# The low part of g in the first block: GpSimd in place of VectorE

## The chip, the cores and the metric

The kernel runs on one core of a Trainium2 chip. The metric is the device time of one execution in microseconds (us). The kernel before took 1154.6 us, the median of three runs (1153.08 to 1154.86). Engines: PE is TensorE (matmuls; PEld its weight loads), DVE is VectorE, ACT is ScalarE, POOL is GpSimd, SP is SyncE, which issues most DMAs.

## The reference

Three layers follow each other, all in float32. Attention works in chunks of 32 queries, each seeing 8 memory keys and a window of 16 + 32 + 8 positions, for 4 batches, 8 heads, 768 positions and a head size of 64. Its output is reshaped to 3072 tokens of 512, and two feed-forward layers follow:

```python
def _moe_ref(x, w_in, w_out):          # x 3072 x 512, w_in 512 x 2048, w_out 2048 x 512
    h = x @ w_in
    g = np.maximum(0.01 * h, h)
    return (g @ w_out).astype(np.float32)

def _moe2_ref(x, w_a, w_b, w_out):     # w_a, w_b 512 x 1536, w_out 1536 x 512
    a = x @ w_a
    b = x @ w_b
    return (a * b @ w_out).astype(np.float32)
```

## The kernel before

TensorE gets its operands split: a float32 value is a high part, the value rounded to float32r by a copy on ScalarE, and a low part, the value less the high part, a subtraction. Each product is three matmuls: low weight by high x, high weight by low x, high by high.

The first feed-forward layer runs over six blocks of 512 tokens (block `bi`, 0 to 5) and in each over 16 slices of 128 hidden units (`f`). An item is one slice of one block. `mm1_pe` makes h (12 matmuls, L412 to L414). `mm1_act` makes g from h on ScalarE (L514) and calls `split_g`: ScalarE casts g to gh (L429), and the subtraction of L430 makes gl. `mm2` multiplies gh and gl with the second weights into four accumulators (12 matmuls, L532, L535, L536). `mm2` of an item comes two items after its `mm1` (`LAG = 2`, list `behind`), so there are two items of matmuls between h and the use of gl.

In block 0 the weights are made as well. A weight arrives as the two 32-bit halves of a float64 pattern. ScalarE scales the high half (L103), VectorE joins the halves in three instructions (L113, L116, L119), ScalarE casts the joined value to the high part (L173), and VectorE subtracts for the low part (L182). Each item of block 0 calls `W1.step()` twice, which makes one first weight (needed by `mm1`) and one second weight (needed by `mm2`). The attention of the next block's four units runs beside the items: scores on TensorE (L276), maxima, differences, sums and products on VectorE (L290, L295, L329 to L332), exponentials on ScalarE (L312), transposes (L356) and the product with v (L385) on TensorE. ScalarE also places q in a padded tile (L248, L249).

The first three items of block 0 have 256 columns, since only half the block's attention is done then; their other halves come as three more items at the end of the block. So block 0 has 3 + 13 + 3 items. The first three are called by `first_items`, where the order on the engines is the written one (class `InOrder`, L31 to L50: each call is issued after the one before; these show the lines L44 and L47 in the profile). After it, `e.on = False`, and the order of each engine's queue is laid out by the framework's planner, which places what it expects to be ready; so instructions of different calls are interleaved in the trace. The queues themselves run in order. GpSimd is called directly, never through `InOrder`, and before the change only for memsets at the start.

The tiles g (tag "t", four buffers), gh and gl (three buffers each) are in SBUF.

Of the kernel before, what the change touches and what calls it, by code (L numbers as in the profile page):

```python
# [53 lines left out]
def kernel(  # L54
# [10 lines left out]
    nc = tc.nc  # L65
# [21 lines left out]
    pe, dve, act, sp = [InOrder(tc, e) for e in (nc.tensor, nc.vector, nc.scalar, nc.sync)]  # L87
# [328 lines left out]
    def proj(ps, slot, x, c):  # L416
        hi, lo = x
        for kc in range(KC):
            mm3(
                ps[:, c],  # L420
                (slot[:, 0, kc * P:kc * P + P], slot[:, 1, kc * P:kc * P + P]),
                (hi[:, kc, c], lo[:, kc, c]),
                kc == 0, kc == KC - 1,
            )

    def split_g(g, c):
        gh = tp.tile([P, TB], F32R, tag="gh", name="gh", bufs=3)
        gl = tp.tile([P, TB], F32R, tag="gl", name="gl", bufs=3)
        act.copy(gh[:, c], g[:, c])  # L429
        dve.tensor_tensor(  # L430
            out=gl[:, c], in0=g[:, c], in1=gh[:, c].bitcast(F32), op=ALU.subtract
        )
        return gh, gl
# [71 lines left out]
    def mm1_pe(bi, parts):  # L505
        ps = ps_h.tile([P, TB], F32, tag="h", name="h")
        for o, n, f in parts:
            proj(ps, wslot[f, 0], x1["x", bi], slice(o, o + n))
        c = slice(min(o for o, _, _ in parts), max(o + n for o, n, _ in parts))
        return ps, c  # L510

    def mm1_act(ps, c):
        g = tp.tile([P, TB], F32, tag="t", name="g")
        act.activation(g[:, c], ps[:, c], AF.Prelu, alpha=0.01)  # L514
        return split_g(g, c)

    def mm1(bi, parts):
        return mm1_act(*mm1_pe(bi, parts))

    def mm2(bi, parts, g):  # L520
        if bi not in acc:
# [32 lines left out]
    for f in range(NF1 + LEAD):  # L554
        if f < LEAD:
            parts = [(0, HALF, f)]
        elif f < NF1:
            parts = [(0, TB, f)]
        else:
            parts = [(HALF, HALF, f - NF1)]  # L560
# [19 lines left out]
    def first_items():  # L580
        parts = [items[f][2] for f in range(LEAD)]
        W1.join()
        a_soft2(2)
        h0 = mm1_pe(0, parts[0])
        g0 = mm1_act(*h0)
        W1.bias(4)
        W1.cast(3)
# [17 lines left out]
        load_v(2)  # L605
        W1.load(13)
        g1 = mm1_act(*h1)
        h2 = mm1_pe(0, parts[2])
        a_turn_mm(3, ps_s, "s")
# [175 lines left out]
    for bi, f, parts in items[LEAD:]:  # L785
# [10 lines left out]
        if first:  # L796
            W1.load(2 * f + 14)
            W1.step()
        behind.append((bi, parts, mm1(bi, parts)))
        if first:  # L800
            W1.step()
# [227 lines left out]
```

## Time and profile before

| | |
|---|---|
| median of three runs | 1154.6 us |
| profiled execution, its own time | 1154.32 us |
| its span | 1152.5 us |
| granted clock of TensorE, mean | 0.998 |
| DVE busy | 665.4 us (58%), 1233 instructions |
| ACT busy | 441.7 us (38%), 734 instructions |
| L430, all blocks | 96 instructions, 65.4 us on DVE |

A row of the timeline gives the start in us from the span's beginning, the duration in us, the engine, the line, the operation, out<-in, shapes and a count, and in brackets the idle time of the engine just before it and what ended that. A row of a stretch gives its length, then busy us and instructions of PE, PEld, DVE, ACT and POOL, TensorE's granted clock, the DMA share and GB/s.

### The profile page before, as it was taken

To read this page: it belongs to the slowest core of one execution; us is meant where nothing else is said; L and a number is where in the kernel's file an instruction comes from. 1 tells how busy PE (TensorE), PEld (TensorE's weight loads), DVE (VectorE), ACT (ScalarE), POOL (GpSimd) and SP (SyncE) were. 2 spreads that over 40 slices of the span, in tenths; PEclk is the share of its full clock that TensorE was granted. 3 is DMA by queue.
4 is the path that set the end of the run, shared out by engine and by line. 5 is a ranking of instruction groups with operands and counts; after the bars stand their busy time and mean duration, and the time that the engine had idled before them with its cause. 6 is when DMAs were issued, how large, how long until landed. Compare 5 with 4: busy or idle time off the path is not lost.

```text
span 1152.5 us, 16036 instructions
## 1 busy us (share of the span) xinstructions
PE 1134.1 (98%) x6344; PEld 938.6 (81%) x6344; DVE 665.4 (58%) x1233; ACT 441.7 (38%) x734; POOL 6.3 (1%) x16
## 2 busy tenths in 40 slices
PE   6899999999999999999999999999999999999998
PEld 6678888888888888888888888888888888888887
DVE  6899489889979834545114433475433465433443
ACT  5787564556455534325223222241222232122210
POOL 2000000000000000000000000000000000000000
PEclk9999999999999999999999999999999999999999
DMA  9977899998999845336248335355544344443413
GB/s 325 354 264 279 308 341 322 317 354 300 330 339 333 298 164 182 111 114 215 92 146 314 144 128 201 128 227 220 208 148 163 146 148 187 185 166 142 186 64 110
DMA packets 68299, 250.67 MB, mean 217 GB/s; under 512 B 7297, under 2 KB 8705, under 8 KB 62849
## 3 DMA queue, kind: packets, MB, share of 16 engines
q1 hardware_dynamic: 67920, 249.33, 60.3%
q8 instruction: 50, 0.82, 0.3%
q10 hardware_dynamic: 304, 0.33, 0.1%
q14 instruction: 25, 0.20, 0.1%
HBM read 200.34 MB, written 49.28 MB: 217 GB/s over the span
## 4 chain that ended last, share of the span: by engine, by line
PE 94%; DVE 0%; DVEq 0%; issue 0%
PE h L412 7%; PE a L532 7%; PE a L536 7%; PE a L535 7%; PE h L414 7%; PE h L413 7%; PE o L925 6%; PE o L927 6%; PE o L926 6%; PE A L860 4%; PE A L859 4%; PE A L858 4%; PE C L858 3%; PE C L860 3%; PE C L859 3%; PE pv L385 2%
## 5 line engine op out<-in xcount | busy, mean ns | idle before, releaser
L412 PE MATMUL h<-xh,w 128*128 128x512 f32 (+1 forms) x384 | 152.1, 396 | 3.1 <-ACT w L47 3.1
L532 PE MATMUL a<-gh,w 128*128 128x512 f32 (+1 forms) x392 | 150.7, 385 | 0.9 <-DVE w L182 0.9
L535 PE MATMUL a<-gl,w 128*128 128x512 f32 (+1 forms) x392 | 150.4, 384 | 0.0
L536 PE MATMUL a<-gh,w 128*128 128x512 f32 (+1 forms) x392 | 150.4, 384 | 0.0
L413 PE MATMUL h<-xl,w 128*128 128x512 f32 (+1 forms) x384 | 149.0, 388 | 0.0
L414 PE MATMUL h<-xh,w 128*128 128x512 f32 (+1 forms) x384 | 148.9, 388 | 0.0
L430 DVE TENSOR_TENSOR gl<-g,gh 128x512 fp32r<-128x512 f32 (+1 forms) x96 | 65.4, 682 | 105.8 <-ACT gh L429 105.6
L925 PE MATMUL o<-w,cl 128*128 128x512 f32 x288 | 112.1, 389 | 0.0
L927 PE MATMUL o<-w,ch 128*128 128x512 f32 x288 | 112.0, 389 | 0.0
L926 PE MATMUL o<-w,ch 128*128 128x512 f32 x288 | 112.0, 389 | 0.0
L514 ACT ACTIVATE g<-h 128x512 f32<-128x512 f32 (+1 forms) x96 | 56.5, 589 | 126.3 <-PE h L414 125.5
L872 ACT COPY u<-A 128x512 f32<-128x512 f32 x72 | 42.3, 588 | 142.2 <-PE A L860 142.2
L412 PEld LDWEIGHTS h<-xh,w 128*128 128x128 f32 x384 | 72.5, 189 | 18.7 <-ACT w L47 3.2
L532 PEld LDWEIGHTS a<-gh,w 128*128 128x128 f32 x392 | 73.7, 188 | 16.3 <-DVE w L182 1.3
L880 DVE TENSOR_TENSOR ga<-u,C 128x512 f32<-128x512 f32 x36 | 24.8, 688 | 106.9 <-ACT u L872 77.7
L536 PEld LDWEIGHTS a<-gh,w 128*128 128x128 f32 x392 | 73.6, 188 | 14.5
L535 PEld LDWEIGHTS a<-gl,w 128*128 128x128 f32 x392 | 73.7, 188 | 14.5
L414 PEld LDWEIGHTS h<-xh,w 128*128 128x128 f32 x384 | 72.4, 189 | 14.8
L859 PE MATMUL A<-cl,wab 128*128 128x512 f32 x216 | 84.1, 389 | 0.0
L858 PE MATMUL A<-ch,wab 128*128 128x512 f32 x216 | 84.0, 389 | 0.0
L860 PE MATMUL A<-ch,wab 128*128 128x512 f32 x216 | 84.0, 389 | 0.0
L413 PEld LDWEIGHTS h<-xl,w 128*128 128x128 f32 x384 | 72.6, 189 | 14.1 <-DVE xl L47 0.3
(138 smaller groups left out, 1918.7 us busy)
## 6 DMA issues: line engine op xcount, KB each, us to landing
wab<-wab SPq DMA_DIRECT2D x36, 1792.0 KB, 7.4
w<-wod SPq DMA_DIRECT2D x116, 512.0 KB, 5.2
raw<-w SPq DMA_DIRECT2D x68, 512.0 KB, 6.9
k<-kl SPq DMA_DIRECT2D x48, 256.0 KB, 5.4
v<-vl SPq DMA_DIRECT2D x48, 256.0 KB, 5.4
wab<-pwb SPq DMA_DIRECT2D x12, 1024.0 KB, 7.7
wab<-pwa SPq DMA_DIRECT2D x12, 768.0 KB, 7.2
wod<-w SPq DMA_DIRECT2D x16, 512.0 KB, 6.1
```

The lines of the kernel that those rows point to most:

```text
L412: pe.matmul(ps, w[1], x[0], start=first, stop=False)
L413: pe.matmul(ps, w[0], x[1], start=False, stop=False)
L414: pe.matmul(ps, w[0], x[0], start=False, stop=last)
L532: pe.matmul(ps, slot[:, 1, c], gh[:, t], start=f == 0 and o == 0, stop=False, **kw)
L535: pe.matmul(ps, slot[:, 0, c], gl[:, t], start=False, stop=False, **kw)
L536: pe.matmul(ps, slot[:, 0, c], gh[:, t], start=False, stop=f == NF1 - 1 or (o == HALF and f == LEAD - 1), **kw)
L858: nc.tensor.matmul(ps, w[:, 1, i, c], hi[:, kc], start=first and kc == 0, stop=False, **kw)
L859: nc.tensor.matmul(ps, w[:, 0, i, c], lo[:, kc], start=False, stop=False, **kw)
L860: nc.tensor.matmul(ps, w[:, 0, i, c], hi[:, kc], start=False, stop=kc == HC - 1, **kw)
L925: nc.tensor.matmul(o, cl[:, q], w[:, 0, :], start=k == 0, stop=False)
L926: nc.tensor.matmul(o, ch[:, q], w[:, 1, :], start=False, stop=False)
L927: nc.tensor.matmul(o, ch[:, q], w[:, 0, :], start=False, stop=k == NCH - 1)
```

## The change

`split_g` takes the engine of the subtraction as an argument. `mm1` passes GpSimd for block 0 and VectorE for the other blocks. The three items of `first_items` call `mm1_act` directly and stay on VectorE. So 16 of the 96 subtractions of L430 move, 13 of 128x512 and 3 of 128x256. All else is as it was.

```diff
-    def split_g(g, c):
+    def split_g(g, c, eng):
         gh = tp.tile([P, TB], F32R, tag="gh", name="gh", bufs=3)
         gl = tp.tile([P, TB], F32R, tag="gl", name="gl", bufs=3)
         act.copy(gh[:, c], g[:, c])
-        dve.tensor_tensor(
+        eng.tensor_tensor(
             out=gl[:, c], in0=g[:, c], in1=gh[:, c].bitcast(F32), op=ALU.subtract
         )
         return gh, gl
...
-    def mm1_act(ps, c):
+    def mm1_act(ps, c, eng=None):
         g = tp.tile([P, TB], F32, tag="t", name="g")
         act.activation(g[:, c], ps[:, c], AF.Prelu, alpha=0.01)
-        return split_g(g, c)
+        return split_g(g, c, eng or dve)
 
     def mm1(bi, parts):
-        return mm1_act(*mm1_pe(bi, parts))
+        return mm1_act(*mm1_pe(bi, parts), nc.gpsimd if bi == 0 else dve)
```

## Rows read from the trace of the kernel before

**Rows 1.** The page: busy time of each engine, share of the span, instructions.
```profile
PE 1134.1 (98%) x6344; PEld 938.6 (81%) x6344; DVE 665.4 (58%) x1233; ACT 441.7 (38%) x734; POOL 6.3 (1%) x16
```
**Rows 2.** Busy time by stretch: us, PE, PEld, DVE, ACT, POOL, clock, DMA, GB/s.
```profile
43.30:59.40 16.10, 15.67 (x106) 12.97 (x105) 13.66 (x25) 12.50 (x19) 0.00 (x0) 1.00 0.92 352
...
69.50:102.50 33.00, 33.00 (x247) 27.29 (x248) 31.90 (x63) 26.66 (x43) 0.00 (x0) 1.00 0.82 276
...
130.00:603.00 473.00, 472.98 (x2985) 391.22 (x2982) 312.09 (x670) 214.12 (x336) 0.00 (x0) 1.00 0.71 248
```
**Rows 3.** Waits of TensorE, 0 to 603 us: total us, times, longest.
```profile
PE h L412 <- ACT w L47: 3.1, 1, 3.1
...
PE a L532 <- DVE w L182: 0.9, 2, 0.5
```
**Rows 4.** Groups of VectorE, 43.3 to 121.1 us: busy us, mean ns, idle before.
```profile
L430 DVE TENSOR_TENSOR gl<-g,gh 128x512 fp32r<-128x512 f32 x13 | 9.0, 693 | 1.4 <-ACT gh L429 1.4
```
**Rows 5.** Timeline, 0 to 8 us: memsets of GpSimd and VectorE.
```profile
0.74 0.98 POOL L212 MEMSET qs<- 64x512 f32 x2 [0.29 <-POOLq L1011]
...
6.72 0.52 POOL L221 MEMSET qz<- 64x512 f32 x1
...
0.91 0.48 DVE L44 MEMSET qs<- 64x512 f32 x1 [0.91 <-PEq L1011]
```
**Rows 6.** Timeline, 44 to 49 us: ScalarE, VectorE, TensorE.
```profile
44.68 0.69 DVE L430 TENSOR_TENSOR gl<-g,gh 128x512 fp32r<-128x512 f32 x1 [1.37 <-ACT gh L429]
...
46.83 1.14 ACT L173 CAST w<-z 128x512 fp32r<-128x512 f32 x2
...
47.48 0.69 DVE L182 TENSOR_TENSOR w<-z,w 128x512 fp32r<-128x512 f32 x1 [0.56 <-ACT w L173]
...
48.23 0.39 PE L532 MATMUL a<-gh,w 128*128 128x256 f32 x1 [0.43 <-DVE w L182]
```
**Rows 7.** Timeline, 54 to 60 us: VectorE, TensorE.
```profile
54.51 0.69 DVE L430 TENSOR_TENSOR gl<-g,gh 128x512 fp32r<-128x512 f32 x1
...
58.31 0.68 DVE L182 TENSOR_TENSOR w<-z,w 128x512 fp32r<-128x512 f32 x1
...
59.26 0.40 PE L532 MATMUL a<-gh,w 128*128 128x512 f32 x1
```
**Rows 8.** Timeline, 59 to 66 us: VectorE, TensorE.
```profile
59.43 0.69 DVE L182 TENSOR_TENSOR w<-z,w 128x512 fp32r<-128x512 f32 x1 [0.43 <-ACT w L173]
...
62.14 0.68 DVE L430 TENSOR_TENSOR gl<-g,gh 128x512 fp32r<-128x512 f32 x1
...
65.22 0.69 DVE L182 TENSOR_TENSOR w<-z,w 128x512 fp32r<-128x512 f32 x1
...
65.96 0.50 PE L532 MATMUL a<-gh,w 128*128 128x512 f32 x1 [0.49 <-DVE w L182]
```
**Rows 9.** Timeline, 67 to 70 us: VectorE, TensorE.
```profile
67.09 0.68 DVE L430 TENSOR_TENSOR gl<-g,gh 128x512 fp32r<-128x512 f32 x1
...
68.30 0.69 DVE L182 TENSOR_TENSOR w<-z,w 128x512 fp32r<-128x512 f32 x1
...
69.40 0.50 PE L412 MATMUL h<-xh,w 128*128 128x512 f32 x1
```
**Rows 10.** Timeline, 101 to 105 us: VectorE, TensorE.
```profile
101.85 0.70 DVE L430 TENSOR_TENSOR gl<-g,gh 128x512 fp32r<-128x512 f32 x1
...
102.52 0.71 DVE L182 TENSOR_TENSOR w<-z,w 128x512 fp32r<-128x512 f32 x1
...
104.19 0.39 PE L532 MATMUL a<-gh,w 128*128 128x512 f32 x1
```
**Rows 11.** Busy time of 40 to 42 us, columns as in rows 2.
```profile
40.00:42.00 2.00, 2.00 (x6) 1.61 (x5) 2.00 (x5) 0.62 (x1) 0.00 (x0) 0.50 0.98 373
```
**Rows 12.** Timeline, 118 to 127 us: ScalarE, TensorE.
```profile
118.64 0.62 ACT L429 CAST gh<-g 128x512 fp32r<-128x512 f32 x1
...
126.80 0.40 PE L535 MATMUL a<-gl,w 128*128 128x512 f32 x1
```

## The prediction

> **What bounds the kernel now.** Read the page's busy shares first: TensorE is busy for 98% of the span and GpSimd for 6.3 us, in 16 instructions [rows 1]. Next come the busy times by stretch. From 130 to 603 us TensorE is busy for 472.98 of 473 us [rows 2], so nothing that happens before 130 us is made good there: a wait added to block 0 moves the end by its own length, and a wait taken away gives back its own length. The third view is TensorE's waits up to 603 us. In the stretch of the change (from 43.3 us on) it lists one pair: 0.9 us in two waits of the second product for the low part of a weight, made by VectorE on L182 [rows 3]. The 3.1 us wait of L412 lies ahead of the change, in the part whose order is written out by hand. So the whole prize in block 0 is 0.92 us. What stands close behind TensorE is VectorE: from 69.5 to 102.5 us it is busy for 31.90 of 33.00 us [rows 2]. In block 0 it joins and splits the weights, does the softmax of four units and makes gl. So its queue is what the change can relieve or burden, and each of its low weight parts has a date at which TensorE needs it.
>
> **What is removed.** The fourth to last items of block 0 are 16: 13 with 512 columns and 3 with 256. VectorE loses 13 subtractions of 693 ns [rows 4]. They overlap their neighbours: from the one at 67.09 to the L182 at 68.30 two instructions start in 1.21 us, so one is worth 0.60 us of the queue [rows 9]. That is 13 x 0.60 = 7.8 us. The three narrow ones come at the end of the block, where VectorE has idle time, and count for nothing. A wait goes as well: at 44.68 VectorE sat idle for 1.37 us because the subtraction at the head of its queue waited for gh [rows 6]; GpSimd now waits for it, with nothing queued behind but later subtractions.
>
> **What is added.** 16 GpSimd subtractions. The trace of before has none. The nearest rows are GpSimd's memsets of 64 x 512, 0.52 us each [rows 5]; a memset only writes. The low bound is therefore 0.52 us, the high bound three such streams, two reads and a write one after the other, 1.56 us. I take two, 1.04 us, as the writes can go along with the reads. By the Trainium skill (GPSIMD Engine Reference, section "Performance versus the Vector engine") a two-input fp32 operation of 2048 elements takes 4497 ns; a quarter of that is an estimate of 1.12 us for one subtraction.
>
> **Is gl late?** The time from the end of gh to the first matmul on gl is shortest for the item whose cast ends at 118.64 + 0.62 = 119.26 us and whose L535 starts at 126.80: 7.54 us [rows 12]. Even 1.56 us plus a wait for a VectorE instruction fits. The cover is the two items by which the second product trails the first. So the added wait of TensorE for GpSimd costs nothing.
>
> **Does VectorE pay?** This decides the sum. If the two engines don't disturb each other, VectorE gains 0.60 us for each subtraction. If VectorE stands still for as long as GpSimd works, it loses 1.04 - 0.60 = 0.44 us for each. The rows show only memsets side by side: GpSimd's pair takes 0.98 us beside VectorE's two of 0.48 us, and neither is stretched [rows 5]; but they read nothing, and a subtraction reads two tiles. I take the second, full standstill, and keep the first as the other end: of the instructions between which GpSimd would have to fit, nearly all of VectorE's in this stretch read tiles in SBUF, back to back.
> The Trainium skill (SBUF — State Buffer, section "SBUF: two separate sides") says that VectorE's operations with two SBUF inputs and GpSimd's reading ones hold a shared port pair by an exclusive lock for a whole instruction, which speaks against this change. No run here shows it yet. By that lock with the 1.12 us above, x below is 0.52 and the sum +1.2 us; without any lock the sum is -0.5 us.
>
> **The sum.** Let x be what VectorE loses for each subtraction (0.44 in the forecast). It reaches TensorE only where a low weight part is due at once. There are five such dates:
> - 48.23 us, a wait of 0.43. The L182 at 47.48 waits for a cast on ScalarE, the second of two from 46.83 on, which stand behind two copies of q [rows 6]. VectorE's load doesn't matter: 0.
> - 59.26 us. The L182 at 58.31 ends at 59.00, 0.26 us early; two subtractions come before it since 47.48, and 0.08 us of idle time [rows 2, 6, 7] (2.44 in all from 43.3 to 59.4, less 1.37, 0.56 and the 0.43 in rows 8). Lag 2x - 0.34 = 0.54. Against it stands the 1.37 us of idle time which the change frees, if the order lets VectorE do later joins in it: 0 with it, +0.54 without. I take 0.
> - 65.96 us, a wait of 0.49 on the L182 at 65.22. Since the idle time that ended at 59.43 there is one subtraction, at 62.14, and no slack [rows 8]: +x = +0.44.
> - 69.40 us. The L182 at 68.30 ends at 68.98, 0.42 early, one more subtraction: x - 0.42 = +0.02 [rows 9].
> - 104.19 us. The L182 at 102.52 ends at 103.23, 0.96 early; five subtractions since, the last at 101.85, and 33.00 - 31.90 = 1.10 us of idle time: 5x - 2.06 = +0.14 [rows 2, 10].
> Other low parts are done over a microsecond ahead with fewer subtractions before them. Sum: 0.44 + 0.02 + 0.14 = +0.60 us. The profiled execution took 1154.32 us (span 1152.5 and 1.8 around it), 0.3 under the median of 1154.6, so the forecast is **1154.9 us**.
>
> **Rivals.**
> 1. *VectorE becomes the bound (slower).* GpSimd's subtraction takes 1.56 us and VectorE stands for all of it: x = 0.96. Then the dates give 1.58 - 1.37 = 0.21, 0.96, 0.54 and 4.80 - 2.06 = 2.74, together +4.45: 1158.8 us. From the third date on the sum is 7x - 2.48, so it passes +2.3 us (0.2%, about what a measurement of this kernel can tell from no change) at x = 0.68, a subtraction of 1.28 us. For it: VectorE is 31.90 of 33.00 us busy. Against: the memset at 0.52. A single wait would stay under the 3.1 us after which the granted clock was 0.50 from 40 to 42 us [rows 3, 11], so no loss of clock is added.
> 2. *The engines don't disturb each other (a little faster).* x = -0.60: the wait at 65.96 goes, -0.49, 1153.8 us; if the casts are ordered otherwise too, -0.92, 1153.4 us. For it: the undisturbed memsets. More than 0.92 us isn't there to be won in block 0.
> 3. *GpSimd is far slower than its memsets suggest,* or finds no gap in VectorE's queue. It decides from the time of an item on TensorE, 6.4 us (six items from 65.96 to 104.19) [rows 8, 10]. At 7 us the 13 items would add some 13 x 0.6 = 7.8: 1162.1 us. For it: the trace shows no such operation. Against: that is over ten times a memset.
> 4. *The order is planned anew and eats the gain:* the rows of before show VectorE's order interleaved from several steps, and with gl gone other steps may go ahead of a low part. One instruction of 0.60 us before a due one costs 0.60: 1154.9 us, as the forecast.
>
> **Chances.** Forecast 0.47 (with rival 4); rival 1 0.28; rival 2 0.20; rival 3 0.05. Within 0.2%: the forecast, 0.16 of rival 2, 0.03 of rival 1 at its lower edge: 0.66. Slower: 0.25 of rival 1 and rival 3: 0.30. Faster: 0.04, if a new order also shortens a wait ahead of the block. The range goes from rival 2's end to rival 1's, 1153.4 to 1158.8; the forecast's own is 1153.8 to 1156.0.
>
> **What will show it.** L430 on GpSimd 16 times and on VectorE 80 times; its duration (right near 1.04 us, rival 1 from 1.28 on). VectorE's instructions that overlap one: stretched or started late against 693 ns by about a microsecond (standstill) or not at all (rival 2). TensorE's waits for L182 in block 0: 0.92 before; some 1.5 in the forecast, 0.43 in rival 2, over 3 in rival 1, with its largest near 104 us. No wait of L535 for GpSimd. The forecast is wrong if TensorE's waits between 43 and 130 us change by over 2.3 us, or if the time moves without them.

## The result and the profile after

The changed kernel took 1163.93 us (median of six runs, 1159.66 to 1167.43) against 1154.78 us (1153.08 to 1155.45) for the one before: a ratio of 1.0077, 95% interval 1.0054 to 1.0101. It is slower by some 9 us, and beyond the range of the prediction. The profiled execution took 1165.23 us, its span 1163.3 us: 10.8 us more than the span before.

The page first. What answers to [rows 1] and [rows 4]: GpSimd's 16 subtractions are there, and TensorE is still busy for 98% of a longer span.

```profile
PE 1138.6 (98%) x6344; PEld 941.9 (81%) x6344; DVE 664.8 (57%) x1217; ACT 439.5 (38%) x734; POOL 37.0 (3%) x32
```

The groups of GpSimd by line and shape (busy us, mean ns of one, idle time before them and what ended it):

```profile
L430 POOL TENSOR_TENSOR gl<-g,gh 128x512 fp32r<-128x512 f32 x13 | 28.5, 2192 | 93.6 <-ACT gh L429 55.1 <-DVE z L119 38.5
L430 POOL TENSOR_TENSOR gl<-g,gh 128x256 fp32r<-128x256 f32 x3 | 2.2, 736 | 10.8 <-ACT gh L429 10.8
```

The mean of 2192 ns hides two things, which the timeline keeps apart. In the rows below (start, duration, engine) the first subtraction runs while VectorE is idle and takes 1.29 us. The one at 70.84 is recorded with 4.62 us: VectorE goes through its queue beside it at its usual pace, an instruction each 0.60 us, until the L182 at 74.23, which takes 1.78 us in place of 0.68. I read this as one and the same subtraction that first waits for its turn; when it has it, VectorE stands still for 1.10 us (1.78 less 0.68). Not every subtraction costs that much: of the 13 wide ones, nine hold a VectorE instruction for 0.93 to 1.10 us, one for 0.33 us, and three (two of them beside an idle VectorE) for nothing. That is 9.8 us in all, 0.76 us each.

```profile
45.72 1.29 POOL L430 TENSOR_TENSOR gl<-g,gh 128x512 fp32r<-128x512 f32 x1 [38.49 <-DVE z L119]
...
70.84 4.62 POOL L430 TENSOR_TENSOR gl<-g,gh 128x512 fp32r<-128x512 f32 x1 [5.39 <-ACT gh L429]
...
72.69 0.68 DVE L116 SCALAR_TENSOR_TENSOR z<-raw,z 128x512 int32<-128x512 int32 x1
73.29 0.41 DVE L113 TENSOR_SCALAR z<-raw 128x512 int32<-128x512 int32 x1
73.63 0.68 DVE L119 SCALAR_TENSOR_TENSOR z<-raw,z 128x512 int32<-128x512 int32 x1
74.23 1.78 DVE L182 TENSOR_TENSOR w<-z,w 128x512 fp32r<-128x512 f32 x1
75.93 0.68 DVE L116 SCALAR_TENSOR_TENSOR z<-raw,z 128x512 int32<-128x512 int32 x1
```

Next TensorE's waits up to 620 us, the view of [rows 3] (total us, times, longest). The L182 waits have grown from 0.9 to 2.1 us, where the forecast had some 1.5. The first line is the one that it hadn't: a single wait of 3.60 us of the transposes (L356) for the softmax (L332). L535 doesn't appear: gl is never late.

```profile
PE pT L356 <- DVE p L332: 3.6, 1, 3.6
PE h L412 <- ACT w L47: 3.1, 1, 3.1
...
PE a L532 <- DVE w L182: 1.6, 3, 0.6
PE a L532 <- ACT x L549: 0.7, 1, 0.7
PE h L412 <- DVE w L182: 0.5, 2, 0.2
```

The timeline around that wait, ScalarE, VectorE, GpSimd and TensorE, shows the chain of one attention unit, its differences (L295), exponentials (L312) and products (L332):

```profile
103.69 0.68 DVE L119 SCALAR_TENSOR_TENSOR z<-raw,z 128x512 int32<-128x512 int32 x1
104.29 0.68 DVE L295 TENSOR_TENSOR p<-s,m 128x512 f32<-128x512 f32 x1
...
104.40 0.62 ACT L173 CAST w<-z 128x512 fp32r<-128x512 f32 x1 [1.77 <-DMA wod<-w]
104.93 1.12 ACT L248 COPY qz<-qr 64x512 f32<-64x512 f32 x1
106.06 1.12 ACT L249 COPY qz<-qr 64x512 f32<-64x512 f32 x1
107.20 0.63 ACT L312 ACTIVATE p<-p 128x512 f32<-128x512 f32 x1
...
109.11 1.52 POOL L430 TENSOR_TENSOR gl<-g,gh 128x512 fp32r<-128x512 f32 x1 [5.38 <-ACT gh L429]
...
109.41 1.25 DVE L330 TENSOR_SCALAR l<-l 128x8 f32<-128x8 f32 x1
...
111.85 0.68 DVE L332 TENSOR_TENSOR p<-p,l 128x512 f32<-128x512 f32 x1
...
112.67 1.09 PE L356 MATMUL pT<-id,p 128*128 128x128 f32 x4 [3.60 <-DVE p L332]
```

L295 is done at 104.97, but the exponentials start only at 107.20: ahead of them on ScalarE stand a cast that waited 1.77 us and two copies of q for the next unit. (The row puts the cast's wait down to a DMA; the L119 that ends at 104.37, 0.03 us before the cast starts, could as well be what it waited for. Which of them it was isn't settled.) Then the small L330, which took 0.18 us before the change, takes 1.25 us beside a GpSimd subtraction. Before the change the same unit had room to spare: the two copies lay ahead of the end of L295, the exponentials started as L295 ended, and L332 ended at 103.80 + 0.71 = 104.51, 2.41 us before the transposes started.

```profile
97.14 1.08 ACT L249 COPY qz<-qr 64x512 f32<-64x512 f32 x1
98.51 0.70 DVE L295 TENSOR_TENSOR p<-s,m 128x512 f32<-128x512 f32 x1
99.25 0.64 ACT L312 ACTIVATE p<-p 128x512 f32<-128x512 f32 x1 [1.03 <-DVE p L295]
...
103.80 0.71 DVE L332 TENSOR_TENSOR p<-p,l 128x512 f32<-128x512 f32 x1
...
106.92 0.60 PE L356 MATMUL pT<-id,p 128*128 128x128 f32 x4
```

ScalarE is only part of the delay. L295 itself is late: it starts 8.4 us ahead of the transposes before the change (98.51 and 106.92), and only 4.8 us ahead of the time at which TensorE is ready for them after it (104.29 and 109.07). Besides the standstills there is an order on VectorE too: L295 is its 159th instruction in the changed kernel, and the 153rd in the old order without the subtractions (sub_oldorder below), so six more instructions of the weights go ahead of it.

The wait has a second price. In the stretches below (columns as in [rows 2]; the granted clock is the number ahead of the DMA share) TensorE was idle from 109.07 to 112.67, and the clock granted from 112 to 118 us is 0.50, the 1.2 GHz level.

```profile
110.00:112.00 2.00, 0.00 (x0) 0.00 (x0) 2.00 (x5) 1.15 (x3) 0.63 (x1) 0.84 1.06 426
112.00:114.00 2.00, 1.33 (x6) 1.26 (x7) 2.00 (x5) 0.84 (x2) 0.00 (x0) 0.50 1.01 414
...
116.00:118.00 2.00, 2.00 (x6) 1.52 (x6) 1.97 (x3) 1.32 (x3) 1.35 (x1) 0.50 0.00 0
118.00:120.00 2.00, 2.00 (x10) 1.62 (x9) 0.50 (x1) 1.22 (x2) 0.00 (x0) 0.96 0.00 0
```

The four transposes take 1.09 us instead of 0.60, and the twelve matmuls of L412 to L414 behind them 5.04 us from the first start to the next group's instead of 2.85. Together that is 2.7 us.

The span's 10.8 us, by how much later each item starts on TensorE than before: 0.8 us is there already at 39 us, ahead of the change (it comes between 22 and 24 us; in this execution the granted clock was 0.50 from 22.6 to 26.0 us, in the one before it was 1.00 there); 1.2 us comes by 106 us, where the waits for L182 are 1.1 us longer in sum; then 3.60 of the wait and 2.8 with the lost clock, 8.4 in all, which stands without change up to 236 us; 1.2 more by 263 us, with the wait of 0.7 for L549; and 1.2 after that.

Last, the instructions' order. Set against before, the queues differ beyond the 16 subtractions. In the recorded orders that the kernels below are held in, an instruction that moved being counted twice (taken out and put in), VectorE's 1217 instructions without the subtractions differ in 220, ScalarE's 720 in 102, SyncE's 453 in 34 and TensorE's 5564 in 22. So up to a tenth of VectorE's and ScalarE's instructions moved, and hardly any of TensorE's.

### The profile page after: what moved, and what is told of

Its sections match the earlier page's. It is cut to its first block, busy times and chain, and to the rows that moved or that the text cites. A ratio compares the mean times of both kernels' runs of the same rounds, so it can differ in the third digit from the quotient of the medians.

```text
span 1163.3 us, 16079 instructions
## 1 busy us (share of the span) xinstructions
PE 1138.6 (98%) x6344; PEld 941.9 (81%) x6344; DVE 664.8 (57%) x1217; ACT 439.5 (38%) x734; POOL 37.0 (3%) x32
## 4 chain that ended last, share of the span: by engine, by line
PE 89%; DVE 3%; DMA 1%; ACT 0%; issue 0%; SPq 0%; DVEq 0%; ACTq 0%
PE h L412 7%; PE a L532 7%; PE a L535 7%; PE a L536 7%; PE h L413 7%; PE h L414 7%; PE o L925 6%; PE o L927 6%; PE o L926 6%; PE A L858 4%; PE A L860 4%; PE A L859 4%; PE C L858 3%; PE C L859 3%; PE C L860 3%; PE pv L385 2%
## 5 line engine op out<-in xcount | busy, mean ns | idle before, releaser
L412 PE MATMUL h<-xh,w 128*128 128x512 f32 (+1 forms) x384 | 153.2, 399 | 3.6 <-ACT w L47 3.1
L532 PE MATMUL a<-gh,w 128*128 128x512 f32 (+1 forms) x392 | 150.8, 385 | 2.3 <-DVE w L182 1.6
L535 PE MATMUL a<-gl,w 128*128 128x512 f32 (+1 forms) x392 | 150.4, 384 | 0.0
L414 PE MATMUL h<-xh,w 128*128 128x512 f32 (+1 forms) x384 | 149.6, 390 | 0.0
L430 DVE TENSOR_TENSOR gl<-g,gh 128x512 fp32r<-128x512 f32 x80 | 55.0, 688 | 100.9 <-ACT gh L429 100.6
L412 PEld LDWEIGHTS h<-xh,w 128*128 128x128 f32 x384 | 73.1, 190 | 19.7 <-ACT w L47 3.2
L532 PEld LDWEIGHTS a<-gh,w 128*128 128x128 f32 x392 | 73.6, 188 | 18.3 <-DVE w L182 2.9
L535 PEld LDWEIGHTS a<-gl,w 128*128 128x128 f32 x392 | 73.7, 188 | 14.4
L414 PEld LDWEIGHTS h<-xh,w 128*128 128x128 f32 x384 | 73.1, 190 | 15.1
```

What stands on the lines that cost most here:

```text
L412: pe.matmul(ps, w[1], x[0], start=first, stop=False)
L414: pe.matmul(ps, w[0], x[0], start=False, stop=last)
L532: pe.matmul(ps, slot[:, 1, c], gh[:, t], start=f == 0 and o == 0, stop=False, **kw)
L535: pe.matmul(ps, slot[:, 0, c], gl[:, t], start=False, stop=False, **kw)
```

## The experiments

My theory after this: the change does two things, it lets VectorE stand still (S), and it brings another order of the queues (O). The expectations call the standstill alone theory A and the order alone theory B. Neither alone is dear; together they use up the slack of the softmax at 107 us, and the wait that follows costs clock as well. Rivals: the standstill alone explains it; the order alone does; or the lost clock does most of it.

To hold an order, the kernels below end with edges that make each instruction of a queue follow its predecessor in the recorded order, on TensorE, VectorE, ScalarE and SyncE, without a semaphore (ORDER lists the instructions of one of the two kernels, queue by queue). Each ratio is to runs of the kernel before taken beside it, and each trace is of one execution:

```python
made = {i.name: i for i in nc.cur_bb.bb.instructions}
for queue in ORDER:
    for a, b in zip(queue, queue[1:]):
        tc.add_manual_dep(
            made[f"I-{b}"], f"I-{a}",
            mybir.DependencyInfo(mybir.DependencyClass.NoSync, mybir.DependencyReason.DATA),
            reason="order",
        )
```

**sub_oldorder**: the changed kernel, its queues held in the order of before. The standstill without the new order.

> The changed kernel (16 subtractions of block 0 on GpSimd), with the queues of TensorE, VectorE, ScalarE and SyncE held in the order that the kernel before has, the subtractions merely gone from VectorE's. Theory A (standstill: VectorE stands still for about 1.1 us whenever GpSimd reads its two tiles) expects most of the loss to stay: 1160 us or more. Theory B (the new order of the queues puts the softmax of the third unit late) expects the loss to go, but for the small waits at the low weight parts: 1154 to 1157 us.

Measured: 1158.60 us against 1155.58, ratio 1.0023 (1.0014 to 1.0031): between the ranges of the two theories. TensorE's waits from 43 to 260 us:

```profile
PE a L532 <- ACT x L549: 1.4, 1, 1.4
PE a L532 <- DVE w L182: 1.2, 3, 0.5
PE pT L356 <- DVE p L332: 0.2, 1, 0.2
PE h L412 <- DVE w L182: 0.2, 1, 0.2
```

In block 0 that is 1.6 us of waits, where the forecast had 1.52 (0.92 and 0.60). The sum agrees, its terms don't: 0.36 us at 49.1 (forecast 0.43), 0.49 at 67.2 (0.93), 0.20 at 70.9 (0.02) and 0.34 at 106.2 (0.14), and 0.21 at 66.1 for a softmax, which the dates don't have. The rest of the 3 us lies outside it: 0.6 us ahead of the change, where the clock of this execution was 0.50 from 22.9 to 26.3 us, and the wait of 1.36 us for L549 at 246.7 us. GpSimd waits for its turn here too: its longest record goes from 108.81 to 115.97 us, 7.16 us, and still no L535 waits.

**mem_oldorder**: as sub_oldorder, but GpSimd only writes zeros (the low part of g is left out): nearly no S, and no O.

```diff
+        if eng is nc.gpsimd: eng.memset(gl[:, c].bitcast(F32), 0.0)
```

> The order of the kernel before on the four queues, and GpSimd only writes zeros to gl in the 16 items (the low part of g is left out there), so it reads nothing. This is VectorE relieved with neither a standstill nor a new order. Both theories expect no loss: 1153.5 to 1155 us, since at most the 0.92 us of waits for L182 can go. Anything slower would show a third cause, such as the start of GpSimd itself.

Measured: 1155.91 us against 1155.58, ratio 1.0003 (0.9994 to 1.0012). TensorE waits 0.11 us in all from 43 to 130 us, against 0.91 before. The time doesn't show those 0.8 us (it is just above the range expected); they are less than this interval tells apart with certainty. Two of the 16 memsets stretched a VectorE instruction, each time L113: 0.77 us at 50.48 and 0.83 us from 93.90, in place of 0.42; no instruction with two inputs was stretched.

**mem_neworder**: the order of the changed kernel, and GpSimd only writes zeros: O nearly without S.

> The order of the changed kernel on all queues, and GpSimd only writes zeros to gl in the 16 items (the low part of g is left out there). Theory A expects the loss to go: 1154 to 1156 us. Theory B expects it to stay, with the wait of L356 for L332 of some 3 us and the half clock behind it: 1160 to 1164 us.

Measured: 1157.23 us against 1155.58, ratio 1.0023 (1.0012 to 1.0034): again between the two theories. In block 0 of the profiled execution TensorE gains: it stands 0.89 us ahead of before at 133 us. The loss comes later, at 244.1 us:

```profile
PE a L532 <- ACT x L549: 1.5, 1, 1.5
PE a L532 <- DVE w L182: 0.6, 1, 0.6
```

So each of S and O costs some 2.7 us by its ratio (3.0 and 1.7 by the medians), and both together 9 us: they don't add up. Neither the standstill nor the order makes the 9 us by itself, and both rivals of that kind fall. In the traces the wait of 3.60 us is there only with both. How much room the softmax at 107 us had agrees: L332 ended 2.41 us ahead of the transposes before, 1.64 us ahead in sub_oldorder and 1.26 us ahead in mem_neworder.

The runs of mem_neworder say that its trace is not the whole of it. Seven of the twelve took 1155.95 to 1157.29 us with a mean granted clock of 0.997 to 0.999, the profiled one (1156.22) among them; the other five took 1158.33 to 1162.29 us, each with 0.996. So in some executions the order alone cost more, and clock too; where, no trace shows.

**sub_narrow**: only the three 256-column items at the end of the block go to GpSimd (the edit is to the changed kernel). No edges are needed: in the traces TensorE's and ScalarE's instructions stand in the order of before, and VectorE's too but for the three.

```diff
-        return mm1_act(*mm1_pe(bi, parts), nc.gpsimd if bi == 0 else dve)
+        return mm1_act(*mm1_pe(bi, parts), nc.gpsimd if bi == 0 and parts[0][1] == HALF else dve)
```

> Only the last three items of block 0 (256 columns) subtract on GpSimd; the other queues keep the order of before. VectorE is idle there. Both theories expect 1154.8 us, within 1 us. If GpSimd's first subtraction or a preparation for it costs TensorE time at the start (in the changed kernel TensorE reached the first wide item 0.8 us later than before), it stays here: 1155.6 us.

Measured: 1154.99 us against 1155.58, ratio 0.9992 (0.9984 to 1.0001). Where VectorE has time, moving the subtraction is free, and wins nothing that can be told from no change.

**after_again**: the changed kernel once more, beside the next three.

> The changed kernel once more, on the chip on which the next three run: 1161 to 1166 us, with a wait of L356 for L332 of some 3.6 us near 110 us. The four kernels of the first experiments gave +3.0 us for the standstill alone and +1.7 us for the order alone; if both only add, this should be 1160 us, and it is the excess over that which the next runs are to place.

Measured: 1164.81 us against 1154.92, ratio 1.0079 (1.0065 to 1.0093), with the 3.60 us wait at 112.7 us again.

**q_ahead**: the changed kernel in its own order but for two instructions: on ScalarE, the copies of q (L248, L249) go ahead of the cast that waited 1.77 us. This tests the chain read above. If it is right, the wait and the lost clock go; GpSimd and VectorE have the same instructions in the same order as in the changed kernel.

The edit, in short (line numbers stand for instructions):

```diff
 ScalarE's order
-  ..., L173, L248, L249, L312, ...
+  ..., L248, L249, L173, L312, ...
```

> The changed kernel with its own order on all queues, but for one place on ScalarE: the two copies of q (L248, L249) that stand behind a weight cast which waited 1.77 us for a DMA now stand ahead of it, so that they run in that wait and the exponential of the third unit (L312) comes earlier. Theory B2 (the softmax of the third unit, late by order and by standstill together, makes the wait of 3.6 us, and the wait the half clock): L312 about 1.8 us earlier, the wait 1.8 us or less, no or little half clock, 1159 to 1161 us. If the excess is spread over the low weight parts instead (theory A2): within 1 us of the changed kernel.

Measured: 1159.62 us, ratio 1.0042 (1.0029 to 1.0055): 5.2 us under after_again, with no overlap of the intervals. ScalarE and the transposes now:

```profile
101.38 1.10 ACT L249 COPY qz<-qr 64x512 f32<-64x512 f32 x1
102.50 0.62 ACT L173 CAST w<-z 128x512 fp32r<-128x512 f32 x1
103.03 0.63 ACT L312 ACTIVATE p<-p 128x512 f32<-128x512 f32 x1
...
109.09 0.63 PE L356 MATMUL pT<-id,p 128*128 128x128 f32 x4 [1.10 <-DVE p L332]
```

The exponentials start 4.2 us earlier, the wait is 1.10 us, and the granted clock from 106 to 120 us is 1.00. TensorE is 2.16 us late at 133 us in place of 8.38. The rest of the loss, 4.7 us by the medians, is in good part later: 1.70 us of wait for L549 at 247.3 us.

The copies are not all of this. They bring the exponentials from 2.23 to 0.34 us after the end of L295, 1.9 us of the 4.2. The other 2.3 us are L295's, which starts at 102.01 in place of 104.29: 0.6 us were gained ahead of the change, and VectorE stood still less. One subtraction here is recorded with 9.52 us, from 70.23 to 79.75, beside which no VectorE instruction is stretched, so that from 70 to 85 us VectorE loses 0.5 us to the standstill in place of 2.2.

**warm**: the changed kernel with 26 matmuls ahead of these transposes whose result isn't used, so that TensorE isn't idle there. It asks what the lost clock is worth.

```diff
+        for _ in range(26 if u == 6 else 0): pe.matmul(ps[:, 0].rearrange("p c q -> p (c q)"), ident, ident, start=True, stop=True)
```

> The changed kernel in its own order, with 26 unused 128x128 matmuls on TensorE ahead of the transposes of the third unit, about 3.3 us long, which fill the wait. If the half clock after the wait is caused by TensorE standing still, the granted clock stays 1.00 and the time falls by about 2.2 us against the changed kernel. If the clock has another cause, or if the matmuls only delay TensorE, the time is the same or longer.

Measured: 1162.70 us, ratio 1.0072 (1.0058 to 1.0085). The clock stayed at 1.00 there, but the matmuls took 5.8 us, longer than the wait that they filled. (In its profiled execution, of 1166.53 us, a later wait of 2.38 us for the accumulators, at 254.0 us, cost clock.) It can't decide the question; warm13 below is the better size.

**copy_oldorder**: the order of before, and GpSimd copies g to gl (one input in SBUF in place of two; the low part of g is left out). It shows whether the standstill needs two inputs.

```diff
+        if eng is nc.gpsimd: eng.tensor_copy(out=gl[:, c], in_=g[:, c])
```

> The order of the kernel before on the other queues, and GpSimd copies g to gl in the 16 items (one tile read in place of two; the low part is replaced there by g itself). If VectorE stands still for as long as GpSimd streams, the copy holds it for less: an operation of 0.6 to 0.8 us in place of 1.29, VectorE's instructions beside it stretched by 0.4 to 0.6 in place of 1.1, and 1155.5 to 1157 us against 1158.6 for the subtraction. If only two-input operations stop VectorE: no stretched instruction and 1155.9 us.

Measured: 1156.79 us against 1154.92, ratio 1.0014 (1.0005 to 1.0022). Its group on GpSimd:

```profile
L430 POOL CAST gl<-g 128x512 fp32r<-128x512 f32 x13 | 14.8, 1139 | 98.1 <-ACT g L513 60.2 <-DVE z L113 37.9
```

A copy takes 0.62 us where nothing is in its way and up to 3.02 us where it waits for its turn. VectorE's L119 at 50.22 beside one takes 1.10 us in place of 0.69: a standstill of 0.4 us. One read is enough to hold a VectorE instruction with two inputs, and for how long goes with the length of GpSimd's instruction (1.10 us beside 1.29, 0.4 beside 0.62).

**q_x_ahead**: q_ahead, and on ScalarE an accumulator copy (L549) moved ahead too, to take away the second wait.

> The changed kernel with the two copies of q moved ahead as before, and one more move on ScalarE: the fourth copy of block 1's first accumulators (L549) stands ahead of the weight cast (L125) which waits near 243 us, as TensorE's L532 then waits for it, 1.70 us near 247 us in the kernel with the copies of q alone. If that second wait is a matter of ScalarE's order too, it goes, and the time is 1.7 us lower: about 1158 us against 1159.6. If the accumulators are late for another reason, the time stays at 1159.6.

Measured: 1159.18 us against 1154.86, ratio 1.0043 (1.0030 to 1.0056), as q_ahead. The copy that I moved belongs to block 0, and the wait at 247 us is for one of block 1, so this says nothing of the second wait. It gave something else. In its profiled execution VectorE stood still between 70 and 85 us as in the changed kernel (2.2 us), L295 started at 103.92, and the exponentials followed its end by 0.32 us. So this trace has the copies' share alone: the wait of L356 is 2.30 us in place of 3.60, and the clock granted behind it still fell, to 0.57 from 112 to 114 us. It fell once more behind a wait of 2.09 us at 251.2 us, to 0.55 from 252 to 254 us. That execution took 1165.34 us; the other runs, of which there is no trace, took 1158.97 to 1161.89 with a mean granted clock of 0.996 to 0.999 in place of 0.994. The copies moved ahead do not make the wait harmless in every execution.

**warm13**: as warm, with 13 matmuls.

> The changed kernel in its own order with 13 unused matmuls ahead of the transposes of the third unit. 26 took 5.8 us, longer than the wait of 3.6 us, and so gave back what the full clock gained; 13 take 2.9 us and fit into the wait. If standing still costs the clock and the half clock costs 2.2 us: granted clock 1.00 throughout, a rest of the wait of some 0.7 us, and 2.2 us less than the changed kernel, about 1162.6 us. If not: 1164.8.

Measured: 1163.25 us, ratio 1.0071 (1.0055 to 1.0087). The clock held at 1.00 up to 120 us, and TensorE is 5.76 us late at 133 us against 8.38: so 2.6 us of the loss in block 0 is the clock's. The time hardly shows this gain: the median is 1.6 us under that of after_again, and the intervals overlap. In the profiled execution (1164.88 us) it is given back at 251.4 us, where L532 (a line further down in this kernel) waits 2.24 us for L549 (0.7 in the changed kernel's profile, 1.81 in that of after_again), and the clock falls with that wait.

```profile
250.00:252.00 2.00, 0.59 (x1) 0.50 (x2) 1.10 (x1) 1.87 (x3) 0.00 (x0) 0.81 0.49 200
252.00:254.00 2.00, 2.00 (x21) 1.35 (x21) 0.73 (x2) 0.00 (x0) 0.00 (x0) 0.50 0.34 131
254.00:256.00 2.00, 2.00 (x22) 1.76 (x20) 1.05 (x2) 1.08 (x1) 0.00 (x0) 0.83 0.41 78
```

**x_ahead**: q_ahead, and this time block 1's own copy (the fourth L549) goes ahead of a cast (L125) that stood before it on ScalarE.

> The changed kernel with the two copies of q ahead, and the fourth copy of block 1's accumulators (the L549 that TensorE's L532 waited for, 1.70 us near 247 us) ahead of the weight cast L125 that waited 1.50 us just before it. The kernel meant to test this before had moved another instance of that line, of block 0. If ScalarE's order makes the wait, the copy starts some 2 us earlier and the wait goes: 1158 us. If the copy is late because its buffer is free only when the DMA of the first copy has landed (issued near 241.0 us, some 5.3 us to land), it starts at 246 us, the wait shrinks by 0.3 us or so, and the time stays at 1159.5 us.

Measured: 1161.08 us against 1155.40, ratio 1.0047 (1.0033 to 1.0061). Of the two times expected it is nearer to the one for a late buffer (1159.5), and above it. The copy is now ahead of the cast, and still late:

```profile
246.27 0.58 ACT L549 COPY x<-a 128x512 f32<-128x512 f32 x1 [2.06 <-DMA x2d<-x]
...
246.91 0.50 PE L532 MATMUL a<-gh,w 128*128 128x512 f32 x1 [1.03 <-ACT x L549]
```

The fourth copy needs the buffer of the first (tag "z" has three), and by the trace it waits for the DMA that stores it. So this wait isn't one of ScalarE's order alone. Before the change the date was tight already: the fourth copy ended 0.18 us before the L532 that needs its accumulator.

```profile
242.25 0.57 ACT L549 COPY x<-a 128x512 f32<-128x512 f32 x1
...
243.00 0.40 PE L532 MATMUL a<-gh,w 128*128 128x512 f32 x1
```

Idle time of TensorE in two stretches, from the busy time of each profiled execution, with that execution's time, and the ratio of all runs:

| kernel | 43 to 130 us | 240 to 270 us | this execution, us | ratio |
|---|---|---|---|---|
| before | 0.91 | 0.00 | 1154.32 | 1 |
| sub_narrow | 0.83 | 0.00 | 1155.74 | 0.9992 |
| mem_oldorder | 0.11 | 0.05 | 1155.18 | 1.0003 |
| copy_oldorder | 0.80 | 0.77 | 1156.70 | 1.0014 |
| mem_neworder | 0.62 | 1.55 | 1156.22 | 1.0023 |
| sub_oldorder | 1.59 | 1.36 | 1158.91 | 1.0023 |
| x_ahead | 2.81 | 1.04 | 1159.35 | 1.0047 |
| q_ahead | 2.91 | 1.70 | 1159.16 | 1.0042 |
| q_x_ahead | 4.25 | 2.09 | 1165.34 | 1.0043 |
| warm13 (matmuls count as busy) | 2.64 | 2.24 | 1164.88 | 1.0071 |
| warm (matmuls count as busy) | 2.05 | 2.38 | 1166.53 | 1.0072 |
| changed kernel | 5.67 | 0.71 | 1165.23 | 1.0077 |
| changed kernel (after_again) | 5.62 | 1.81 | 1167.23 | 1.0079 |

The order by the first two columns is nearly that by the execution's time. Where it isn't, in warm13 and warm, the matmuls that fill the wait and the clock lost with the second one are missing from the table; in q_x_ahead the ratio is of all runs, and the median of those lies 6 us under the execution with the trace.

## Why the prediction was wrong

Its steps, one by one:

- **The subtraction's duration held roughly.** 1.04 us was forecast, within 0.52 and 1.56; alone it takes 1.29, just past the 1.28 from which the prediction would have read rival 1 (x is not 0.68 even so, see the next point). By the Trainium skill's figure (GPSIMD Engine Reference, "Performance versus the Vector engine") the estimate was 1.12 us; the trace's 1.29 is above it.
- **VectorE stands still: right where it does, but not for each subtraction.** A VectorE instruction that is held loses 1.10 us, which makes x 1.10 - 0.60 = 0.50 there, where the forecast had 0.44. Over the 13 wide subtractions the loss is 0.76 us each, so x is 0.16 on the mean. The lock of which the Trainium skill tells (SBUF — State Buffer, "SBUF: two separate sides") agrees in kind with the L182 of 1.78 us; its loss of 1.10 us is somewhat less than the 1.29 us of a subtraction alone. That the one-input L113 is stretched too (1.53 us at 50.75 in place of 0.41) agrees with the same page of the Trainium skill, section "Who interferes with whom", which counts tensor_scalar among the forms that can take the shared ports. The prediction's reading that memsets disturb nothing [rows 5] holds for those rows, but not for L113 beside a memset (0.77 us in mem_oldorder).
- **gl is never late: right,** though with less to spare than thought. The cover was 7.54 us [rows 12] for a subtraction of about a microsecond; with VectorE's queue in front of it the longest record is 4.62 us, 7.16 us in the old order and 9.52 us in q_ahead, longer than that cover was; even there no L535 waits.
- **The five dates and their sum: near in the old order, and partly by luck.** sub_oldorder waits 1.6 us in block 0, the forecast was 1.52. But the date that should have grown by x, 65.96, waits 0.49 us as before, and 0.21 us is a softmax that the list lacks. In its own order the changed kernel waits 2.1 us for L182, on other dates (49.1, 53.9, 67.0, 70.7 and 90.2 us).
- **The step that failed is rival 4,** "One instruction of 0.60 us before a due one costs 0.60: 1154.9 us, as the forecast". A new order was seen as possible and priced at one instruction, and only low weight parts were looked at for what may come late. The date that broke isn't in the list of five: the transposes at 106.92 us, which need the softmax. It had 2.41 us of slack in the old order. In the new one the copies of q and a cast stand ahead of its exponentials, and six more instructions of the weights ahead of its L295; in that order VectorE's standstill makes it 3.60 us late. The traces of mem_neworder (no such wait without the standstill), of sub_oldorder (0.2 us at another softmax without the new order) and of q_x_ahead (2.30 us with the two copies moved ahead) show each part of this; q_ahead (1.10 us, 5.2 us won by the medians) shows the copies together with a standstill that fell elsewhere.
- **"So no loss of clock is added" fell with it.** That was argued from single waits under 3.1 us. A wait of 3.60 us came, and the clock behind it cost 2.7 us. The threshold that the sentence suggests is wrong too: the clock fell to its lower level behind waits of 2.38, 2.30, 2.24 and 2.09 us as well, and behind the 1.81 us in after_again (from 254.5 to 258.0 us).
- **Nothing was expected behind 130 us.** TensorE's 472.98 of 473 us [rows 2] was read as if no date were near there. It says only that none was missed. The L549 at 242.25 had 0.18 us to spare, and every kernel here but sub_narrow and mem_oldorder waits there, for 0.7 to 2.4 us.

Open: the block starts 0.8 us later in the changed kernel's trace because of the clock from 22.6 to 26.0 us; the same loss stands in five other traces (sub_oldorder, copy_oldorder, after_again, warm, warm13) and not in the rest, whatever their order, so it belongs to the execution and not to the change. What brings the clock down there wasn't looked for. How much the late stores to x2d and how much the order of the queues make of the second wait wasn't told apart. What lets GpSimd's subtraction in at one VectorE instruction and not at another is open too; it differs between q_ahead and q_x_ahead, whose VectorE queues are the same.

The changed kernel's runs also spread wider (7.8 us) than those of before (2.4 us), and the spread goes with the clock: in order of their times, 1159.66 to 1167.43 us, the mean granted clock of the six is 0.997, 0.997, 0.995, 0.994, 0.994 and 0.993. So the 2.7 us of lost clock are those of one execution; others lost less or more, and behind which waits isn't known. No version here beat the kernel before: the nearest, sub_narrow, can't be told from it.

## What to carry to other kernels

Where a planner lays out the queues, moving one instruction to another engine is a change of every queue: ask for every date in the stretch, the softmax and the stores too, how much slack it has, before you price the new order at one instruction. An engine at 98% says that no date was missed, not that none is near. GpSimd is no free helper beside a VectorE that is busy with tiles in SBUF: moving 7.8 us of VectorE's queue there made VectorE stand still for 9.8 us, and the 13 subtractions that kept VectorE busy for 9.0 us took 28.5 us in GpSimd's records.

## What the hardware did that I had not expected

- GpSimd's instruction waits for its turn. While VectorE's queue runs back to back at 0.60 us an instruction, GpSimd's record grows to 4.62 us (7.16 in sub_oldorder, 9.52 in q_ahead) and VectorE isn't slowed; once GpSimd gets its turn, most often one VectorE instruction loses 0.9 to 1.1 us at one stroke.
- A VectorE instruction of 128x8 with one input was held as well: L330 took 1.25 us in place of 0.18. A reduction of the scores (L290) beside a waiting GpSimd instruction was not stretched (0.68 us).
- GpSimd's copy with one input makes VectorE stand too, for 0.4 us. Its memsets left VectorE's memsets alone [rows 5], but two of the 16 in mem_oldorder held the one-input L113 for 0.35 and 0.4 us.
- TensorE's clock fell to the 1.2 GHz level behind waits of 3.60, 2.38, 2.30, 2.24, 2.09 and 1.81 us, and stayed at 1.00 behind 1.70 and 1.10 us (q_ahead). Behind the first it cost 2.6 to 2.8 us (2.6 by warm13, 2.7 by the stretched matmuls, 2.8 by TensorE's delay) on top of the wait of 3.60.
